# First batch of a Fourier mixer with a maxout FFN: six pieces of weights asked for on ScalarE's DMA queue among the pieces of x

## The chip, the cores and the metric

One core of one Trainium2 chip. The metric is device time in microseconds (us) of one execution of the whole kernel, as the median of several runs.

## What is computed

The inputs are x (8 x 3072 x 256), two mixing matrices and two biases, three up-projections and one output matrix (these four come as 64-bit floats, since they are made by a product of a 32-bit array with a 64-bit scalar). The reference, cut to what matters:

```python
X = np.fft.rfft(x, axis=1)                       # along the 3072 positions
Yr = Xr @ w_r - Xi @ w_i + b_r                   # 256 x 256, complex
Yi = Xr @ w_i + Xi @ w_r + b_i
Y  = sign(Y) * max(|Y| - 0.01, 0)                # both parts apart
y  = np.fft.irfft(Y, n=3072, axis=1).astype(np.float32)
x  = y.reshape(8 * 3072, 256)
h  = max(max(x @ w1, x @ w2), x @ w3)            # 256 -> 768, three times
out = h @ w_out                                  # 768 -> 256
```

## The kernel before

The Fourier transform over 3072 positions is split into a transform over 48 rows and one over 64 columns, with 256 channels kept side by side. The eight batches go through it one after the other; while the tokens of one batch run through the feed-forward part (names pu, pq, pw, pd, most of the kernel's time), the Fourier part of the next is mixed in. Matrices of the main part are split into a high and a low half in 16-bit floats, three products for one.

The **first batch** has nothing to be mixed with, so the kernel begins with its Fourier part alone, in 32-bit floats. This head takes about the first hundred microseconds and has these steps:

- `load_x(q)`, q from 0 to 7 (DMA at L701, for the last piece two halves at L697): one eighth of x, 384 KB, on SyncE's (SP) queue. Only a few tiles are free, so five of the pieces land in parts of tiles that serve later for something else: mb_all twice, wuh, wul and ga_sb; the others in xq_c and xr.
- `stage_a(q)`: two matmuls with the 48-row transform (L746, pa<-x, fr), a copy of half the result by ScalarE (ACT, L747) and of the other half by VectorE (DVE, L748) into a tile `aq` or a borrowed one (wch, wcl, wuh, wul and zq_c stand for aq of pieces 2 to 6), and a store to the scratch a_d in HBM, issued by ScalarE (L749).
- `load_a(k)` (L786, aj<-a_d, on SP's queue): reads rows of a_d across all eight pieces, so the first one waits until all eight stores have landed.
- `first_b(k)`: the 64-column transform (L812, px<-aj, mb_all), copied by ScalarE into tf (L817 and L820). `first_w(k)`: mixing (L838 and L839, py<-tf, wst), then bias and threshold on DVE and ACT (L843 to L849, uf). `first_q(k)`: the first step back (L860, pz<-uf, qf), copied to zs and stored to z_d by ScalarE (L1013, L1014). These three run over 25 values of k.
- after that pi (L1081) reads z_d back as zq_c, scaled and split into zh (ACT, L347) and zl (DVE, L348), and the main part begins.

Meanwhile the **up weights** are prepared. They are twelve pieces of 128 rows x 384 64-bit floats (384 KB each, tile rw), a first half of six and a second half of six. `Weights.load(n, queue=nc.sync)` (L507, its DMA at L515) asks for one on the queue that it is given. `join_half(v)` prepares a half on DVE and ACT: per piece the largest value (L519), the fraction (L549, L552), then, after one exponent for the half is known (a transpose L436 into pt and some small DVE operations, L434 to L534), exponent and combination (DVE L559, ACT L562 into r, DVE L566 and L569). `Mix` then forms differences of the three projections (DVE L622), and splits them in high and low (ACT L342 into wuh, DVE L343 into wul); pieces that are needed the other way round are turned on TensorE (PE) (L575, pt<-id_sb, rw).

What sets the order of work: SP's and POOL's instructions at the head stay in program order. On PE, DVE and ACT a planner in the kernel file orders the instructions of the head by costs and due times when the program is built, `holds` keeping some behind others (`join_half(0)` is called after `stage_a(5)`, and its first PE instruction is held behind that stage's). Each engine then works strictly in that order: an instruction that waits holds up all behind it. Every hardware DMA, from whichever engine it is issued, also takes one of eight completion counters (DMAHW0 to DMAHW7), handed out in turn, and its issue waits until the transfer that had the same counter before has landed.

Of the kernel before, what the change touches and what calls it, by code (L numbers as in the profile page):

```python
# [312 lines left out]
def fourier_maxout_kernel(  # L313
    ctx: ExitStack, tc: tile.TileContext, x, w_r, w_i, b_r, b_i, w1, w2, w3, w_out, fa, ga, mb, mq, ident, out
):
    nc = tc.nc
# [44 lines left out]
    def ff_tile(name):  # L361
        tag = spare[0]
        if len(spare) > 1:
            spare.append(spare.pop(0))
        return ps.tile([P, 512], F32, name=name, tag=tag, bufs=PS[tag])
# [27 lines left out]
    def raw_tile(name):  # L393
        return ffn.tile([P, 768], F32, name=name, tag="raw", bufs=14)
# [18 lines left out]
    def load_first_bias():  # L413
        rows = [b.rearrange("(o d) -> o d", o=1) for b in (b_r, b_i)]
        for j in range(2):
            for c in range(2):
                nc.gpsimd.dma_start(
                    out=bias[64 * c:64 * c + 64, j, :], in_=rows[c].broadcast_to([64, D])
                )
        nc.gpsimd.dma_start(out=bias[64:65, 1, :], in_=rows[0])  # L420
        nc.gpsimd.dma_start(out=qf, in_=mq[:, 0:2])
# [181 lines left out]
    w_up = Weights("u", up_parts, 119.0)  # L603
# [78 lines left out]
    def first_rows(q):  # L682
        return slice(32 * (q % 2), 32 * (q % 2) + 2 * N1)

    def clear(t, rows):
        if rows.start:
            nc.gpsimd.memset(t[0:rows.start], 0.0)

    def load_x(q):
        b, q4 = divmod(q, NCH)  # L690
        xv = x[b].rearrange("(n1 q r n) d -> q r n1 (n d)", n1=N1, r=2, n=4)[q4]
        rows = first_rows(q)
        if q == NCH - 1:
            pairs = [raw_tile("xr")[0:rows.stop, 0:2 * D] for _ in range(2)]
            for c, t in enumerate(pairs):
                clear(t, rows)
                nc.sync.dma_start(out=t[rows], in_=xv[:, :, c * 2 * D:c * 2 * D + 2 * D].rearrange("r n1 d -> n1 r d"))  # L697
        elif b == 0:
            xq = x_homes.pop(0) if q in (0, 1, 4, 5, 6) else xqs[q % 2]
            clear(xq, rows)  # L700
            nc.sync.dma_start(  # L701
                out=xq[rows], in_=x[b].rearrange("(n1 q n) d -> q n1 (n d)", n1=N1, n=8)[q4]
            )
            pairs = [xq[0:rows.stop, c * 2 * D:c * 2 * D + 2 * D] for c in range(2)]
        else:
            xq = xqs[0]
            xqs.reverse()
            if q in (NCH, NCH + 1):
                nc.gpsimd.memset(xq[32:64], 0.0)
            for r in range(2):  # L710
                nc.sync.dma_start(out=xq[64 * r:64 * r + N1], in_=xv[r])
            pairs = [xq[0:XR, c * 2 * D:c * 2 * D + 2 * D] for c in range(2)]
            st["xq", q] = xq[0:XR]
        st["x", q] = pairs
# [470 lines left out]

    for q in range(NCH):
        load_x(q)
        if q == 1:
            nc.sync.dma_start(out=id_sb, in_=ident)
    load_first_bias()  # L1190
    for n in range(6):
        w_up.load(n)
    warm = ff_tile("pt")
    for _ in range(2):
        nc.tensor.matmul(warm, zq[32:64, 0:P], zq[32:64, 0:512], start=True, stop=True)
# [17 lines left out]
    for q in range(NCH):  # L1213
        split_x(q)
        stage_a(q)
        if q == 5:
            placed = nc.cur_bb.bb.instructions
            n = len(placed)
# [51 lines left out]
    for q in (NCH, NCH + 1):  # L1270
        n = len(nc.cur_bb.bb.instructions)
# [94 lines left out]
```

## Time and profile before

| | |
|---|---|
| runs (3) | 1737.45, 1737.54, 1738.77 us; median 1737.54 |
| the profiled execution | 1739.03 us, of which its span 1737.2 us |
| mean granted TensorE clock | 0.992 of full speed |
| PE busy, share of the span | 1684.9 us, 97% |
| DVE, ACT, POOL busy | 75%, 69%, 10% |
| the chain that ended last, by engine | PE 87%, DVE 6%, ACT 3%, issue 2%, DMA 2% |

The span runs from the first to the last instruction of the core; some 1.8 us of the execution's time lie outside it. "Busy" says how long an engine worked at all; the chain of waits says what the end of the program was waiting for, step by step backwards. With PE at 97%, nearly all that is not PE lies in the first 130 us.

### The profile page before, as it was taken

How to read it: one execution, taken by the hardware profiler on the slowest of the kernel's cores; microseconds unless marked ns; L12 is line 12 of the kernel's file. 1: busy time of each engine (PE TensorE's matmuls, PEld its weight loads, DVE VectorE, ACT ScalarE, POOL GpSimd, SP SyncE). 2: the span in 40 equal slices, each digit the busy share in tenths (PEclk: the TensorE clock that was granted, in tenths of full speed). 3: DMA queues.
4: the chain of work that ended last, by engine and by line, in shares of the span. 5: the costliest groups of instructions: out<-in, count | busy, mean ns of one | idle time of the engine just before them, and what ended most of it. 6: DMA issues, size and time to landing. Idle time of an engine off the chain costs nothing.

```text
span 1737.2 us, 38864 instructions
## 1 busy us (share of the span) xinstructions
PE 1684.9 (97%) x15509; PEld 1210.4 (70%) x15509; DVE 1295.3 (75%) x2241; ACT 1198.8 (69%) x2279; POOL 174.8 (10%) x200
## 2 busy tenths in 40 slices
PE   6989999999999999999999999999999999999998
PEld 3856767677676767767776777767777677776676
DVE  5988698678867878678886788768886697856542
ACT  2778687677766877577766777667776677656663
POOL 2000001111011111011111101111101111101110
PEclk8989999999999999999999999999999999999999
DMA  9645353434433433334333444333442233221111
GB/s 307 201 131 164 107 153 90 112 95 125 114 101 101 113 103 107 103 107 121 109 103 87 117 121 120 86 102 108 114 119 83 80 92 86 71 71 37 39 32 32
DMA packets 134996, 185.26 MB, mean 107 GB/s; under 512 B 17776, under 2 KB 113264, under 8 KB 134816
## 3 DMA queue, kind: packets, MB, share of 16 engines
q1 hardware_dynamic: 72784, 106.86, 22.9%
q10 hardware_dynamic: 61824, 75.52, 14.6%
q8 instruction: 122, 2.00, 0.5%
q14 instruction: 58, 0.48, 0.1%
q0 software_dynamic: 208, 0.39, 0.1%
HBM read 87.03 MB, written 75.50 MB: 94 GB/s over the span
## 4 chain that ended last, share of the span: by engine, by line
PE 87%; DVE 6%; ACT 3%; issue 2%; DMA 2%; ACTq 0%; SPq 0%; DVEq 0%
PE pd L353 9%; PE pd L354 9%; PE pd L355 9%; PE pq L353 4%; PE pw L353 4%; PE pw L355 3%; PE pw L354 3%; PE pq L355 3%; PE pq L354 3%; PE pu L353 3%; PE pu L355 3%; PE pu L354 3%; PE pa L756 3%; PE pi L1081 3%; PE py L353 2%; PE py L355 2%
## 5 line engine op out<-in xcount | busy, mean ns | idle before, releaser
L353 PE MATMUL pd<-woh,hh 128*128 128x256 f16 x1152 | 314.1, 273 | 0.6 <-ACT o L1174 0.6
L354 PE MATMUL pd<-wol,hh 128*128 128x256 f16 x1152 | 314.0, 273 | 0.0
L355 PE MATMUL pd<-woh,hh 128*128 128x256 f16 x1152 | 314.0, 273 | 0.0
L1150 DVE SCALAR_TENSOR_TENSOR h<-pq,c 128x384 f32<-128x384 f32 x192 | 106.8, 556 | 163.8 <-PE pq L355 133.5
L343 DVE TENSOR_TENSOR hh<-h,hh 128x768 f16<-128x768 f32 x192 | 189.4, 987 | 37.6 <-ACT hh L342 36.8
L355 PEld LDWEIGHTS <-wul 128*128 128x128 f16 x1344 | 131.3, 98 | 92.3 <-issue 5.5
L353 PEld LDWEIGHTS <-wuh 128*128 128x128 f16 x1344 | 131.3, 98 | 90.3 <-issue 28.4
L354 PEld LDWEIGHTS <-wuh 128*128 128x128 f16 x1344 | 131.4, 98 | 89.1 <-issue 33.6
L342 ACT ACTIVATE hh<-h 128x768 f16<-128x768 f32 x192 | 160.3, 838 | 37.1 <-DVE h L1150 33.0
L1103 POOL TENSOR_TENSOR ys<-yt 128x384 f32<-128x384 f32 x62 | 70.1, 1130 | 1114.2 <-ACT yt L1086 1114.2
L1132 ACT ACTIVATE m<-pw 128x384 f32<-128x384 f32 x192 | 93.8, 489 | 113.2 <-PE pw L355 107.9
L1135 DVE TENSOR_TENSOR pq<-pu,m 128x384 f32<-128x384 f32 x192 | 108.4, 565 | 75.8 <-ACT m L1132 74.4
L1138 ACT ACTIVATE r<-pw 128x384 f32<-128x384 f32 x192 | 94.0, 489 | 98.3 <-PE pw L355 87.9
L353 PE MATMUL pw<-yo,wuh 128*128 128x384 f16 x384 | 125.4, 326 | 12.6 <-ACT m L1132 8.1
L353 PE MATMUL pq<-yo,wuh 128*128 128x384 f16 x384 | 125.3, 326 | 8.1 <-DVE pq L1135 5.4
L354 PEld LDWEIGHTS <-hh 128*128 128x128 f16 x1152 | 112.7, 98 | 27.9 <-issue 0.8
L353 PEld LDWEIGHTS <-hh 128*128 128x128 f16 x1152 | 112.7, 98 | 27.6
L354 PE MATMUL pw<-yo,wuh 128*128 128x384 f16 x384 | 125.1, 326 | 2.4 <-DVE yo L343 2.4
L354 PE MATMUL pu<-yo,wuh 128*128 128x384 f16 x384 | 125.2, 326 | 1.9 <-DVE yo L343 1.9
L353 PE MATMUL pu<-yo,wuh 128*128 128x384 f16 x384 | 125.5, 327 | 0.0
L355 PE MATMUL pu<-yo,wul 128*128 128x384 f16 x384 | 125.2, 326 | 0.0
L355 PE MATMUL pw<-yo,wul 128*128 128x384 f16 x384 | 125.1, 326 | 0.0
(280 smaller groups left out, 4514.8 us busy)
## 6 DMA issues: line engine op xcount, KB each, us to landing
z_d<-zs ACTq DMA_DIRECT2D x96, 256.0 KB, 2.5
out_dram<-o ACTq DMA_DIRECT2D x192, 128.0 KB, 2.4
zq_c<-z_d SPq DMA_DIRECT2D x126, 192.0 KB, 3.4
aj<-a_d SPq DMA_DIRECT2D x90, 256.0 KB, 3.0
xq_c<-in_x_dram SPq DMA_DIRECT2D x112, 192.0 KB, 3.5
a_d<-aq ACTq DMA_DIRECT2D x112, 192.0 KB, 3.0
vq<-vp SPq DMA_DIRECT2D x308, 64.0 KB, 2.3
rw<-in_moe_w_dram SPq DMA_DIRECT2D x12, 384.0 KB, 7.2
```

The lines of the kernel that those rows point to most:

```text
L342: nc.scalar.activation(out=hi, in_=src, func=AF.Copy)
L343: nc.vector.tensor_tensor(out=lo, in0=src, in1=h, op=ALU.subtract)
L353: nc.tensor.matmul(o, lh, rh, start=start, stop=False, **kw)
L354: nc.tensor.matmul(o, lh, rl, start=False, stop=False, **kw)
L355: nc.tensor.matmul(o, ll, rh, start=False, stop=stop, **kw)
L756: nc.tensor.matmul(pa[r][64 * c:64 * c + 64], fr[rows], xs[c][rows], start=True, stop=True)
L1081: nc.tensor.matmul(pi[p][:, o:o + N1], lz[r, n2, h * P:(h + 1) * P], ga_sb[r, lg, c * NQ + n2, :], start=lz is zh and lg == 0, stop=lz is zl,)
L1103: (nc.vector if first else nc.gpsimd).tensor_tensor(out=o, in0=x0, in1=x1, op=op)
L1132: nc.scalar.activation(out=m5, in_=pw, func=AF.Copy)
L1135: nc.vector.tensor_tensor(out=pq, in0=pu, in1=m5, op=ALU.add)
L1138: nc.scalar.activation(out=r1, in_=pw, func=AF.Relu, scale=-H_SCALE)
L1150: nc.vector.scalar_tensor_tensor(out=h32[:, n], in0=o, scalar=scale, in1=c, op0=ALU.mult, op1=ALU.max)
```

## The change

In the loop that asks for the eight pieces of x, each of the first six calls of `load_x` is now followed by a request for one piece of the first half of the up weights, on ScalarE's queue. The loop that asked for the same six on SP's queue, behind all of x and the bias, is gone. Sizes, tiles and arithmetic are the same.

```diff
     for q in range(NCH):
         load_x(q)
+        if q < 6:
+            w_up.load(q, nc.scalar)
         if q == 1:
             nc.sync.dma_start(out=id_sb, in_=ident)
     load_first_bias()
-    for n in range(6):
-        w_up.load(n)
     warm = ff_tile("pt")
```

The planner then orders other engines' work differently as well, up to about 200 us. Behind that PE's order is the same, instruction by instruction, and POOL's is the same throughout. In the listings below, numbers tell tiles of one name apart, and the brackets name the counters that an instruction waits for (DMAHW: a DMA; PE_49, DVE_49 and so on: an engine).

On **ScalarE at the very start**, this is the difference (+ is the changed kernel):

```order
 L1361 UNCONDITIONAL_BRANCH
+L515 DMA rw<-in_moe_w_dram 128x768 x5
 L747 ACT_TABLE_LOAD
 L747 ACTIVATE aq<-pa 96x512
-L749 DMA a_d<-aq 48x2x1024
```

Five of the six requests stand ahead of everything that ScalarE does; the sixth stands behind its first copy. The stores of the eight results pa follow. Before, ScalarE's copies and stores at L747 and L749 stood so:

```order
L747 ACTIVATE aq_142<-pa_143 96x512 [waits PE_49]
L749 DMA a_d_149<-aq_142 48x2x1024 [waits DVE_49,Activation_49]
L747 ACTIVATE aq_151<-pa_152 128x512 [waits PE_49]
L749 DMA a_d_149<-aq_151 48x2x1024 [waits DMAHW1_49,DVE_49,Activation_49]
L747 ACTIVATE wch_76<-pa_159 96x512 [waits PE_49]
L749 DMA a_d_149<-wch_76 48x2x1024 [waits DMAHW3_49,DVE_49,Activation_49]
L747 ACTIVATE wcl_77<-pa_166 128x512 [waits PE_49]
L749 DMA a_d_149<-wcl_77 48x2x1024 [waits DMAHW7_49,DVE_49,Activation_49]
L747 ACTIVATE wuh_78<-pa_173 96x512 [waits PE_49]
L749 DMA a_d_149<-wuh_78 48x2x1024 [waits DMAHW1_49,DVE_49,Activation_49]
```

In the changed kernel:

```order
L747 ACTIVATE aq_142<-pa_143 96x512 [waits PE_49]
L515 DMA rw_116<-in_moe_w2_dram 128x768 [waits DMAHW4_49]
L747 ACTIVATE aq_151<-pa_152 128x512 [waits PE_49]
L749 DMA a_d_149<-aq_142 48x2x1024 [waits DMAHW6_49,DVE_49,Activation_49]
L749 DMA a_d_149<-aq_151 48x2x1024 [waits DMAHW0_49,DVE_49,Activation_49]
L747 ACTIVATE wch_76<-pa_159 96x512 [waits PE_49]
L749 DMA a_d_149<-wch_76 48x2x1024 [waits DMAHW3_49,DVE_49,Activation_49]
L747 ACTIVATE wcl_77<-pa_166 128x512 [waits PE_49]
L749 DMA a_d_149<-wcl_77 48x2x1024 [waits DMAHW7_49,DVE_49,Activation_49]
L747 ACTIVATE wuh_78<-pa_173 96x512 [waits PE_49]
L749 DMA a_d_149<-wuh_78 48x2x1024 [waits DMAHW3_49,DVE_49,Activation_49]
L747 ACTIVATE wul_79<-pa_180 128x512 [waits PE_49]
```

The first store moved behind the second copy, and the store of wuh now waits for counter 3, which the store of wch uses two stores ahead of it, where it waited for counter 1.

On **DVE around the two last copies of stage a** (zq_c for piece 6, aq_266 for piece 7), before:

```order
L519 TENSOR_REDUCE mwu_93<-rw_119 128x1
L549 TENSOR_SCALAR m5_188<-rw_119 128x384
L552 SCALAR_TENSOR_TENSOR rw_119<-rw_119,m5_188 128x384
L748 COPY zq_c_86<-pa_260 96x512
L519 TENSOR_REDUCE mwu_93<-rw_121 128x1
L559 TENSOR_SCALAR c1_223<-rw_119 128x384
L549 TENSOR_SCALAR m5_192<-rw_121 128x384
L748 COPY aq_266<-pa_268 128x512
```

In the changed kernel (the pieces of weights are rw_97, rw_101, rw_105, rw_109, rw_112 and rw_116):

```order
L559 TENSOR_SCALAR c1_235<-rw_105 128x384
L748 COPY zq_c_86<-pa_260 96x512
L566 SCALAR_TENSOR_TENSOR r1_224<-rw_97,r1_224 128x384
L569 SCALAR_TENSOR_TENSOR rw_97<-rw_97,r1_224 128x384
L566 SCALAR_TENSOR_TENSOR r1_230<-rw_101,r1_230 128x384
L559 TENSOR_SCALAR c1_241<-rw_109 128x384
L566 SCALAR_TENSOR_TENSOR r1_236<-rw_105,r1_236 128x384
L569 SCALAR_TENSOR_TENSOR rw_101<-rw_101,r1_230 128x384
L748 COPY aq_266<-pa_268 128x512
L569 SCALAR_TENSOR_TENSOR rw_105<-rw_105,r1_236 128x384
```

Between the two copies stand now three combinations of weights (L566), two L569 and one L559, where one maximum, one exponent mask and one fraction stood.

On **ScalarE between the last two stores of stage a and the first tf**, before:

```order
L749 DMA a_d_149<-zq_c_86 48x2x1024 [waits DMAHW7_49,DVE_49,Activation_49]
L747 ACTIVATE aq_266<-pa_267 128x512 [waits PE_49]
L347 ACTIVATE qh_71<-qf_70 128x256 [waits DMASW5_49]
L749 DMA a_d_149<-aq_266 48x2x1024 [waits DMAHW3_49,DVE_49,Activation_49]
L562 ACTIVATE r1_224<-c1_223,bwu0_221 128x384 [waits DVE_49]
L562 ACTIVATE r1_230<-c1_229,bwu0_221 128x384
L562 ACTIVATE r1_236<-c1_235,bwu0_221 128x384 [waits DVE_49]
L817 ACTIVATE tf_296<-px_291 128x4x128 [waits PE_49]
L820 ACTIVATE tf_296<-px_291 128x4x64
```

In the changed kernel:

```order
L749 DMA a_d_149<-aq_266 48x2x1024 [waits DMAHW6_49,DVE_49,Activation_49]
L562 ACTIVATE r1_242<-c1_241,bwu0_221 128x384
L562 ACTIVATE r1_248<-c1_247,bwu0_221 128x384 [waits DVE_49]
L347 ACTIVATE qh_71<-qf_70 128x256 [waits DMASW5_49]
L562 ACTIVATE r1_254<-c1_253,bwu0_221 128x384 [waits DVE_49]
L342 ACTIVATE wuh_78<-rw_109 128x384 [waits DMAHW3_49,DVE_49]
L342 ACTIVATE wuh_78<-rw_112 128x384 [waits DMAHW1_49,DVE_49]
L342 ACTIVATE wuh_78<-rw_116 128x384 [waits DVE_49]
L342 ACTIVATE wuh_78<-rw_97 128x384 [waits DVE_49]
L342 ACTIVATE wuh_78<-rw_101 128x384 [waits DVE_49]
L817 ACTIVATE tf_296<-px_291 128x4x128 [waits PE_49]
L820 ACTIVATE tf_296<-px_291 128x4x64
```

Three more r (L562), and five splits wuh<-rw (L342), which before came after the first tf's, stand ahead of the first tf now.

## Rows read from the trace of the kernel before

**Rows 1.** The page's first line: the span of the profiled execution.
```profile
span 1737.2 us, 38864 instructions
```
**Rows 2.** Chain of waits, 15 to 50 us: start us, us, what.
```profile
15.19 6.96 DMA a_d<-wch
...
27.01 5.66 DMA a_d<-aq
32.69 2.58 DMA aj<-a_d
35.40 3.76 PE px L812 x16
39.16 0.68 PE py L838 x2
...
42.86 0.89 PE px L812 x8
...
49.18 0.43 PE py L838 x2
```
**Rows 3.** Windows: us, PE, PEld, DVE, ACT, POOL busy (count), PEclk, DMA share, GB/s.
```profile
5.00:10.00 5.00, 4.65 (x6) 1.63 (x6) 0.40 (x1) 0.59 (x1) 2.67 (x5) 1.00 1.05 261
23.00:25.00 2.00, 0.14 (x1) 0.00 (x0) 1.99 (x5) 0.29 (x1) 0.00 (x0) 1.00 1.03 415
25.00:30.00 5.00, 0.00 (x0) 0.00 (x0) 4.54 (x12) 0.61 (x2) 0.00 (x0) 0.59 1.03 385
...
39.20:100.00 60.80, 60.80 (x306) 50.61 (x309) 57.98 (x175) 43.87 (x86) 0.94 (x1) 1.00 0.55 184
105.00:110.00 5.00, 1.38 (x10) 0.53 (x3) 5.00 (x12) 3.49 (x8) 0.00 (x0) 0.78 0.74 184
110.00:115.00 5.00, 4.25 (x22) 3.60 (x20) 5.00 (x12) 2.38 (x4) 0.00 (x0) 0.50 0.82 203
```
**Rows 4.** DMA queues, 3 to 15 us: packets, MB, share of 16 engines.
```profile
q1 hardware_dynamic: 955, 2.85, 92.7%
q0 software_dynamic: 128, 0.26, 8.9%
```
**Rows 5.** DMA issues at 10.4 and 72.9 us: count, KB, us from issue to landing.
```profile
a_d<-aq ACTq DMA_DIRECT2D x1, 384.0 KB, 7.3
...
z_d<-zs ACTq DMA_DIRECT2D x1, 256.0 KB, 2.1
```
**Rows 6.** ScalarE in order of time, 24 to 38 us: start us, us, line, out<-in [idle before].
```profile
24.13 0.54 ACTq L749 DMA_DIRECT2D a_d<-zq_c  x1
24.71 0.60 ACT L747 ACTIVATE aq<-pa 128x512 f32<-128x512 f32 x1 [2.05 <-DMA a_d<-wcl]
...
37.49 0.60 ACT L817 ACTIVATE tf<-px 128x512 f32<-128x512 f32 x1 [2.25 <-PE px L812]
```
**Rows 7.** Waits of SP, 0 to 45 us: us in total, times, longest.
```profile
SPq L515 <- DMA a_d<-wch: 5.9, 1, 5.9
```
**Rows 8.** DVE in order of time, 34 to 48 us.
```profile
34.51 0.55 DVE L566 SCALAR_TENSOR_TENSOR r<-rw,r 128x384 uint32<-128x384 uint32 x1
34.98 0.35 DVE L559 TENSOR_SCALAR c<-rw 128x384 uint32<-128x384 uint32 x1
...
47.32 0.55 DVE L519 TENSOR_REDUCE mwu<-rw 128x1 f32<-128x384 f32 x1 [0.48 <-DMA rw<-in_moe_w_dram]
```
**Rows 9.** DVE and PE in order of time, 114 to 121 us, and ScalarE's zh before it.
```profile
111.70 1.15 ACT L347 ACTIVATE zh<-zq_c,s0u 112x1024 f16<-112x1024 f32 x1
...
114.27 1.28 DVE L348 SCALAR_TENSOR_TENSOR zl<-zq_c,s0u,zh 112x1024 f16<-112x1024 f32 x1
...
115.60 0.22 PE L1081 MATMUL pi<-ga_sb,zl 48*128 48x48 f16 x2 [0.69 <-DVE zl L348]
116.59 2.93 PE L575 MATMUL pt<-id_sb,rw 128*128 128x128 f32 x12
120.31 0.26 PE L1081 MATMUL pi<-ga_sb,zh 48*128 48x48 f16 x4
```

## The prediction
> **What bounds the kernel now.** I read the page's busy shares first, then the chain of waits, then windows, then single engines in order of time. The span is 1737.2 us [rows 1] and PE is busy in 97% of it, so a change at the head can only move what PE loses there. From 39.2 to 100 us PE is busy 60.80 of 60.80 us [rows 3], with DVE busy in 57.98 of them: whatever delays the first py is still there at 100 us, since nothing in that stretch can be made up. Two places have slack: the time before the first py, and 105 to 120 us, where PE is busy 1.38 and 4.25 of 5 us while DVE is busy all the time [rows 3].
>
> The chain before the first py [rows 2] is one of transfers: a store of stage a, the last store a_d<-aq (asked for at 27.01, landed 32.67), the first aj (2.58), px from 35.40, py from 39.16. The windows say why a store took 5 to 7 us: the DMA share is 1.05 and 1.03, so all engines move data without a break [rows 3], x at 261 GB/s and weights and stores at 415. A piece of 384 KB (393 KB in thousands) is so worth 1.5 us as x and 0.95 as a weight or a store.
>
> In which order transfers move decides the case. The first store a_d<-aq, on ScalarE's queue, took 7.3 us [rows 5] from its issue at 10.4, and from 3 to 15 us the queue q10 (ScalarE's) has no row at all: only SP's q1 and POOL's q0 moved bytes [rows 4]. That store waited for pieces of x that had been asked for before it. With an empty queue a store of 256 KB takes 2.1 us [rows 5]. So I take transfers to move in the order in which they were asked for, whichever queue they are on.
>
> **The change, part by part.**
>
> *Six requests on ScalarE instead of SP.* An issue takes about 0.55 us of the engine [rows 6]. Five stand ahead of all that ScalarE does, but it has nothing to copy before the first piece of x has landed and been transformed: free. SP loses six issues, among them one that waited 5.9 us for a store's counter [rows 7], so SP is free earlier: nothing, because what it asks for next (mb_all, wst) is used only from px on.
>
> *The weights' bytes move ahead of x and the stores.* The store of wch landed at 15.19 + 6.96 = 22.15 [rows 2], and two of the six weight pieces had moved before it. Now all six stand ahead: four pieces more, 4 x 0.95 to 1.0, so it lands at about 26.2. The total of bytes is the same, so this alone would cost nothing for the last store; what makes it cost is a counter. In the changed order of ScalarE the store of wuh waits for counter 3, which the store of wch holds. The engine works in order, so at 26.2 it still has this to do: store wuh 0.55, copy wul 0.60, store 0.55, one r 0.60, copy zq_c 0.60 (durations: [rows 6], r as a copy). DVE's half of zq_c stands behind an L559 that waits for that r (28.5), so it is ready at about 29.6; store zq_c until 30.2, two more r until 31.45. DVE has six weight instructions between its last two copies; the third L566 waits for the r of 31.45, and then L566, L569 and the copy (0.47 apart [rows 8], the copy about 0.7, an estimate from ScalarE's 0.60 for the same shape) end at 33.2. The last store goes out at 33.2 instead of 27.01. By then the queue is empty: 2.1 [rows 5] and 0.35 for the larger piece, landed 35.7 (before 32.67); plus 2.58 for aj, px starts at **38.3, 3.0 later**.
>
> *tf behind five splits.* Before, tf stood only behind px (it waited 2.25 us for it [rows 6]). Now five wuh<-rw stand in front, and the last of them needs DVE's weight work up to its difference L622: 18 instructions behind the copy of 33.2, 0.47 apart and the two L559 among them 0.3 [rows 8], 8.2 us; then the split. tf starts at 41.9 instead of 37.49, and the first py as long after it as before (39.16 - 37.49, less the 0.6 for which py waited on px's end), at 42.95 to 43.2: **4.0 later**. px lies beside this and costs nothing.
>
> *The exponent of the second half.* pt (L436) now stands before the first pz instead of behind the px that follows it. It needs the maximum of the last piece of the second half, which came in at 47.3 [rows 8]; SP asks for it behind the aj's, so some 3 later, 50.3. With the small steps behind it, the py that stood at 49.18 [rows 2] starts at 53.7: **4.5 later in all**, and that goes on to 100 us.
>
> *The clock.* From 25 to 30 us PE has no work and the granted clock is 0.59 on average, on its way to 0.50 of full speed, the lower of the two levels (1.2 GHz) [rows 3]. So 16 px took 3.76 us where 8 take 0.89 later, and the return came at about the end of px: the first two py took 0.68 us, two later ones 0.43 [rows 2]. Now px ends at 42.1 and PE waits 0.9 us before py. From 110 to 115 us PE was busy 4.25 of 5 us and the clock stayed at 0.50 [rows 3], so such gaps can hold it down. Lowest cost: nothing, if it returns as early after px starts as before. Highest: 4.6, if it stays down until the gap at pt is past (9.2 us at half speed). The row with gaps is the nearest one: about 4 us of py at half speed, **+2**.
>
> *The end of the head.* About 10 us of DVE work on the first half is done before py instead of beside it. From 105 to 115 us DVE is busy all the time [rows 3]. The first zl (114.27) starts 1.4 us after its zh has ended (111.70 + 1.15) because wcl, wol and sd stand before it [rows 9]: up to 1.4, taken as 1.1. Between the first and the second pi stand turns of weights, 2.93 us from 116.59 [rows 9]; the second zl, 117.89 + 1.28 [rows 9], holds the second pi back to 119.2 anyway, and it starts at 120.31: 1.1. Together **-2.3**. Bounds: -0.5, if zh alone sets the time, and -5, if PE has no long gap at 105 and so keeps its clock up.
>
> **Sum:** 4.5 + 2 - 2.3 = 4.2. The profiled execution took 1739.03 us, 1.8 of it outside the span, so it would take 1743.2; the median of the runs is 1.5 below it, 1737.54, which gives 1741.7. A measurement of this kernel tells 0.2%, 3.5 us, from no change, so the bounds are 1734.0 and 1741.0.
>
> **Rivals.**
>
> *The two queues share the engines.* Then weights beside x take half the rate from the start, but stores are not held behind x: the store of wch lands at about 20, and ScalarE is no longer bound by the counter but by piece 6 of x. That lands when seven pieces at 1.5, six weights at 0.95 and 1.5 us of tables and bias have moved from 3 us on, 20.7, and its copy follows 2 us later, 22.9 with its matmuls. All of the above comes 3.3 us earlier: 4.5 - 3.3 + 2 - 2.3, about 1738.5, no change that can be told. Against it stand 7.3 us for the first store and the missing q10 [rows 4, 5]: it moved nothing while SP's queue had work. The Trainium skill ("DMA: Bandwidth & Descriptors", Queues, rings and completion order) says that each DMA engine goes round between the queues that have work; by that rule this rival is the forecast, and the trace does not agree before 15 us. The same page (Issuing engines are not separate DMA queues) says that issuing from several engines saves only issue time, which speaks against a gain from the second queue; no row here contradicts that. 0.2.
>
> *DVE's relief decides; the time falls.* The mechanism is the stretch 105 to 120. If the planner's shift takes enough weight work off DVE there that the first pi follows its zh at once and PE never idles 2 us, the clock stays up: at 110 to 120 some 8.6 us of PE work ran at half speed, of which most would be saved, 4 us, beside the 2.3. It decides where the delay of the first py is under 2.5 us, thus where the last store goes out by about 30.5 (as it would if the wait for counter 3 ended three us earlier). Then 1.0 to 2.5 - 2.3 - 4: about 1733. For it: DVE busy all through that stretch [rows 3]. Against it: the gap at 105 to 110, PE busy 1.38 of 5 [rows 3], is a round trip of z_d through HBM, which no DVE work is part of. 0.17.
>
> *The clock stays down for all of the first py's.* As the highest price above: 2.6 more, 1744.3. For it, the 0.50 from 110 to 115; against it, PE has no gaps from 39.2 on [rows 3]. 0.13.
>
> *Nothing changes.* The pieces land early, but the chain of stores through x is as it was, with the order's effects cancelling: about 1737.5. Against it the counter, which stands in the order. It shares the middle with the first rival; 0.1 beside the 0.2.
>
> **How the numbers follow.** Forecast 0.4, spread of its terms -2 to +1.5 us on each, so that about a fifth of it falls under 1741.0. Slower: 0.32 + 0.13 = 0.45. Within 0.2%: 0.08 from the forecast, 0.2 and 0.1 = 0.38. Faster: 0.17. The range from 1734.0 to 1745.0 leaves out most of the third part of the cases on the fast side and the longest of the clock's. The likeliest case alone, slower, spans 1740 to 1744.5.
>
> **What would show it.** Right: the store of wch lands at 26 and the store of wuh is issued just then; the last store of stage a is issued at 33 (before 27.0); the first aj lands, and px starts, at 38 (35.4); five splits stand before tf, at 42 (37.5); the py of 49.18 starts at 53.7; q10 moves the weights early and in turn with x; a row of granted clock below 1.00 behind 43 us. At the end zl follows its zh at once. Wrong: stores that land within 3 us of their issue while x still moves (then the queues share); a last store before 30 us; px's start within 1 us of before; or PE with less idle time between 105 and 120 us than the 2.3 us allow.

## The result, and the profile after

The changed kernel is slower: median 1747.53 us over 4 runs (1746.54 to 1749.54) beside 1737.55 us for the kernel before (4 runs, 1737.45 to 1738.77); ratio 1.0056, 95% interval [1.0041, 1.0072]. The medians are 10.0 us apart; the profiled execution took 1748.35 us, 9.3 more than that of before. The forecast was 1741.7, with a range up to 1745.0: the direction was right, the size was not.

One correction to the description ahead: the steps first_b, first_w and first_q run over 12 values of k, not 25. No number rests on it.

The page of the changed kernel begins (compare [rows 1]):

```profile
span 1746.6 us, 38866 instructions
```

Its chain of waits over the first 60 us (start us, us, what; compare [rows 2]):

```profile
0.73 4.48 DMA rw<-in_moe_w_dram
5.23 11.94 DMA xq_c<-in_x_dram
...
17.31 10.46 PE pa L746 x16
...
35.67 3.28 DMA a_d<-aq
...
54.83 0.49 PE pt L436 x2
...
57.07 0.43 PE py L838 x2
```

The chain now begins with a weight and waits 12 us for a piece of x, and pa stands on it with 10.46 us. The last store goes out at 35.67 (27.01 before), and the py that stood at 49.18 stands at 57.07, 7.9 later.

Windows of the changed kernel (columns as in [rows 3]):

```profile
5.00:10.00 5.00, 1.27 (x2) 0.39 (x2) 2.47 (x6) 1.28 (x1) 2.71 (x5) 1.00 1.04 263
10.00:15.00 5.00, 5.00 (x8) 1.70 (x6) 2.02 (x5) 1.19 (x2) 0.00 (x0) 1.00 1.05 277
...
19.00:21.00 2.00, 2.00 (x4) 0.82 (x3) 0.00 (x0) 0.59 (x1) 0.00 (x0) 0.50 1.04 304
45.00:50.00 5.00, 5.00 (x20) 4.28 (x20) 4.38 (x12) 1.96 (x5) 0.00 (x0) 0.70 1.05 392
110.00:115.00 5.00, 4.72 (x30) 3.04 (x30) 3.21 (x14) 3.33 (x7) 0.00 (x0) 1.00 0.63 184
...
130.00:140.00 10.00, 8.66 (x31) 2.80 (x28) 6.43 (x9) 6.10 (x11) 0.00 (x0) 0.50 0.65 172
```

and, of the kernel before, one window that was not shown and the queues of a window that was (23 to 25 us):

```profile
130.00:140.00 10.00, 9.79 (x105) 4.69 (x103) 8.88 (x13) 8.80 (x18) 0.00 (x0) 1.00 0.67 182
...
q10 hardware_dynamic: 226, 0.79, 97.7%
q1 hardware_dynamic: 18, 0.04, 5.4%
```

Three things stand in these rows. From 5 to 15 us the DMA engines are as full as before, but move 263 to 277 GB/s although about half of it is weights, which alone moved at 374 (e6 below). The 415 GB/s of 23 to 25 us, at which the prediction priced a weight [rows 3], were stores: 0.79 of 0.83 MB came from ScalarE's queue. From 19 to 21 us TensorE does stage a at half speed. And at the end of the head the lower clock has moved: before it lay on 110 to 115 us [rows 3], now these are at 1.00 and the lower clock lies on 130 to 140, on 8.66 us of TensorE's work, most of it feed-forward matmuls.

The queues of the changed kernel from 3 to 15 us (compare [rows 4]), and the issue of its first store at 14.4 us (compare [rows 5]):

```profile
q10 hardware_dynamic: 663, 1.81, 51.7%
q1 hardware_dynamic: 566, 1.40, 44.2%
q0 software_dynamic: 128, 0.26, 8.1%
...
a_d<-aq ACTq DMA_DIRECT2D x1, 384.0 KB, 9.3
```

Both queues move bytes in turn, yet a store still takes 9.3 us behind x and weights. SP was not freer for its six requests less: its requests for x stood 5.8 us behind counters that weights held, which the prediction did not count (the DMA engines were full all the same).

ScalarE and DVE between 28 and 45 us (start us, us, line, out<-in; compare [rows 6]):

```profile
28.52 0.54 ACTq L749 DMA_DIRECT2D a_d<-wuh  x1
...
34.92 0.68 DVE L748 COPY aq<-pa 128x512 f32<-128x512 f32 x1
...
35.67 0.54 ACTq L749 DMA_DIRECT2D a_d<-aq  x1
...
44.36 0.57 ACT L817 ACTIVATE tf<-px 128x512 f32<-128x512 f32 x1
```

The store of wch went out at 21.81 and landed 6.6 us later, at 28.4; the store of wuh follows it at once, as the counter in the order says. DVE's last copy ends at 35.60, TensorE had its operand ready at 31.4: the copy came over 3 us later, behind the weight instructions between the two copies.

TensorE at the places that the runs below compare (compare [rows 9]):

```profile
17.31 7.01 PE L746 MATMUL pa<-xq_c,fr 96*96 96x512 f32 x8 [2.14 <-DMA xq_c<-in_x_dram]
...
41.98 2.05 PE L812 MATMUL px<-mb_all,aj 128*128 128x128 f32 x8 [10.57 <-DMA aj<-a_d]
...
45.53 1.06 PE L838 MATMUL py<-wst,tf 128*128 128x256 f32 x2
...
109.97 1.12 PE L860 MATMUL pz<-uf,qf 128*128 128x512 f32 x2 [1.16 <-DVE mxu L849]
...
115.95 1.68 PE L575 MATMUL pt<-id_sb,rw 128*128 128x128 f32 x12 [1.18 <-DVE wcl L580]
118.09 1.68 PE L575 MATMUL pt<-id_sb,rw 128*128 128x128 f32 x12 [0.47 <-DVE wcl L580]
120.39 0.97 PE L575 MATMUL pt<-id_sb,rw 128*128 128x128 f32 x6 [0.61 <-DVE mb_all L580]
121.39 0.22 PE L1081 MATMUL pi<-ga_sb,zh 48*128 48x48 f16 x4
...
130.06 0.50 PE L353 MATMUL pu<-yo,wuh 128*128 128x384 f16 x1
```

The kernel before has the first py, the last pz and the first pu here:

```profile
38.95 0.89 PE L838 MATMUL py<-wst,tf 128*128 128x256 f32 x2
...
102.08 1.12 PE L860 MATMUL pz<-uf,qf 128*128 128x512 f32 x2 [1.16 <-DVE mxu L849]
...
122.41 0.34 PE L353 MATMUL pu<-yo,wuh 128*128 128x384 f16 x1
```

The first py starts 3.55 us behind px in both: the five splits in front of tf cost it nothing. The 9.3 us arise in four stretches: px 41.98 - 35.40 = 6.6; px to the last pz 1.3 more (109.97 - 102.08 = 7.9); pz to the first pu 20.09 beside 20.33, 0.2 back; pu to the end of the span 1616.5 beside 1614.8, 1.7 more.

### The profile page after: what moved, and what is told of

Its sections match the earlier page's. It is cut to its first block, busy times and chain, and to the rows that moved or that the text cites. A ratio compares the mean times of both kernels' runs of the same rounds, so it can differ in the third digit from the quotient of the medians.

```text
span 1746.6 us, 38866 instructions
## 1 busy us (share of the span) xinstructions
PE 1691.5 (97%) x15509; PEld 1209.8 (69%) x15509; DVE 1296.4 (74%) x2241; ACT 1199.5 (69%) x2279; POOL 176.2 (10%) x200
## 4 chain that ended last, share of the span: by engine, by line
PE 86%; DVE 6%; ACT 4%; issue 2%; DMA 2%; ACTq 0%; SPq 0%; DVEq 0%
PE pd L353 9%; PE pd L355 8%; PE pd L354 8%; PE pq L353 4%; PE pw L353 4%; PE pw L355 3%; PE pw L354 3%; PE pq L355 3%; PE pq L354 3%; PE pu L353 3%; PE pu L355 3%; PE pu L354 3%; PE pa L756 3%; PE pi L1081 3%; PE py L353 2%; PE py L355 2%
## 5 line engine op out<-in xcount | busy, mean ns | idle before, releaser
L342 ACT ACTIVATE hh<-h 128x768 f16<-128x768 f32 x192 | 160.4, 838 | 36.1 <-DVE h L1150 32.8
```

Of the source, the lines that this page charges most:

```text
L342: nc.scalar.activation(out=hi, in_=src, func=AF.Copy)
```

## The experiments

Each kernel ran beside the kernel before, whose medians in the four groups of runs were 1737.98 to 1738.79; the ratio is to those of its own group. px, the last pz and the first pu are TensorE's starts in the profiled execution, "span" is its span. One execution of each kernel was profiled, and its time is not always near the median.

| kernel | px | last pz | first pu | span | median us | ratio, 95% interval |
|---|---|---|---|---|---|---|
| before | 35.40 | 102.08 | 122.41 | 1737.2 | 1737.55 | |
| changed | 41.98 | 109.97 | 130.06 | 1746.6 | 1747.53 | 1.0056 [1.0041, 1.0072] |
| e1 both on SP | 39.00 | 106.89 | 125.42 | 1744.6 | 1747.73 | 1.0049 [1.0034, 1.0064] |
| e2 prepared behind x | 38.66 | 106.16 | 126.00 | 1745.1 | 1746.15 | 1.0038 [1.0023, 1.0053] |
| e3 two pieces | 36.81 | 105.09 | 127.37 | 1745.7 | 1744.15 | 1.0029 [1.0017, 1.0041] |
| e4 ScalarE, behind stages | 37.44 | 104.19 | 123.84 | 1738.3 | 1740.28 | 1.0017 [1.0007, 1.0026] |
| e5 all late | 32.23 | 103.31 | 125.60 | 1742.9 | 1744.45 | 1.0034 [1.0021, 1.0046] |
| e6 weights first | 40.62 | 109.13 | 128.56 | 1746.8 | 1748.09 | 1.0059 [1.0044, 1.0074] |
| e7 extra pa | 41.11 | 113.43 | 133.72 | 1752.6 | 1748.74 | 1.0067 [1.0047, 1.0087] |
| e8 before, extra pa at 105 | 35.30 | 102.95 | 124.74 | 1740.0 | 1740.74 | 1.0017 [1.0007, 1.0026] |
| e9 turns doubled | 41.80 | 110.34 | 131.00 | 1746.7 | 1748.95 | 1.0068 [1.0051, 1.0085] |
| e10 two late | 34.58 | 104.46 | 123.76 | 1740.9 | 1742.75 | 1.0026 [1.0016, 1.0036] |
| e11 e2 and e7 | 37.75 | 105.38 | 125.13 | 1743.1 | 1747.65 | 1.0051 [1.0037, 1.0065] |
| e12 turns as before | 40.63 | 108.58 | 126.37 | 1740.7 | 1743.98 | 1.0028 [1.0017, 1.0039] |
| e13 e2 and e12 | 39.02 | 106.15 | 124.42 | 1738.0 | 1740.89 | 1.0011 [1.0001, 1.0020] |

### Bytes or queue

**e1**, the changed kernel with `w_up.load(q)` in place of `w_up.load(q, nc.scalar)`.

> The six weight pieces asked for at the same places of the loop, but on SP's queue. Theory 1 (the bytes ahead of x are the cost, not the queue): x still ends late, its last half at 25 to 28 us instead of 17.9, the first px at 38 to 42 instead of 35.4, and the time is 1742 to 1748. Rival (sharing between two queues is the cost): with one queue x and weights move in order without loss; x's last half at 24 to 25, px within 2 us of before, time 1737 to 1740.

x ended later still: its last half was asked for at 22.71 and took 6.6 us, 29.3 (27.7 in the changed kernel: 19.32 and 8.3). px came 3.6 late, not within 2, and the time is that of the changed kernel: what moves ahead of x costs on either queue. But the loss does not lie where it lay. px is 3.0 earlier than in the changed kernel, although x ended 1.6 later: the planner put one combination of weights between DVE's last two copies, where the changed kernel has six weight instructions, and the last store went out at 32.86. That was lost again behind the first pu, 1619.2 us to the end beside 1616.5. The granted clock was 0.50 there from 130 to 135 us, and for some 3 us more at 348 and at 1573 us:

```profile
130.00:135.00 5.00, 4.67 (x17) 1.35 (x16) 2.38 (x2) 1.93 (x3) 0.00 (x0) 0.50 0.59 159
```

**e4**, the requests on ScalarE's queue, but in the second loop:

```diff
         stage_a(q)
+        if q < 6:
+            w_up.load(q, nc.scalar)
```

> The six requests on ScalarE's queue, but each behind the stage of its own piece of x; the planner puts two of them ahead of the first stores and four behind the last store. If the queue is innocent and only the bytes' place counts: x is late by one or two pieces (last half at 19 to 20.5), the last store at 27 to 28, px at 34 to 36, and the four late pieces delay the end of the head by 1 to 3 us: 1738 to 1742, clearly below the changed kernel. If a request on ScalarE's queue in itself holds its stores up: px at 38 or later, 1744 and more.

1740.28, as expected if the queue itself does not cost, and clearly below the changed kernel. px, at 37.44, fits neither expectation (34 to 36, or 38 and more). Only two of the six pieces move ahead of the stores here, so this run says less of the bytes than of the requests.

**e6**, the kernel before with all six pieces asked for on SP ahead of the first x.

> All six weight pieces asked for on SP's queue ahead of the first piece of x, so that weights and x do not alternate. Theory M (alternating weights with x makes the weights' bytes move at x's rate): unmixed, the six weights are in by 9 to 10 us at 0.95 each and x ends at 24 to 25 (before 17.9 plus six), earlier than the 27.7 of the changed kernel and the 29.3 of the run with both on SP. Theory N (the early microseconds are slow whatever moves): x ends at 27 to 29 here too. The time is 1741 to 1748 either way, since px comes 4 to 7 late.

Theory M holds. Windows of e6, the first with weights alone:

```profile
4.00:9.00 5.00, 1.51 (x2) 0.00 (x0) 3.92 (x10) 0.00 (x0) 3.77 (x7) 1.00 1.00 374
14.00:19.00 5.00, 5.00 (x7) 1.95 (x8) 0.77 (x2) 0.59 (x1) 1.08 (x2) 1.00 1.04 264
```

Weights alone move at 374 GB/s in the same early microseconds, and x ends at 24.4 (17.09 and 7.3), 3.3 to 4.9 us before the runs in which the two alternate. So a weight piece among x costs what x costs or a little more (x's end moved by 9.8 us for six pieces in the changed kernel, 1.6 each), and ahead of x, unmixed, 1.1. The time is no better for it: the first x lands later, stage a begins at 13.96, and the store of wcl goes out at 27.30 (25.90 in the changed kernel).

**e3**, two of the six pieces as in the change (`if q < 2`), four as before.

> Only the first two pieces of weights on ScalarE's queue beside x, the other four on SP behind x as before. Theory 1: x is late by two pieces, 2 to 3 us (last half at 20 to 21 instead of 17.9), and the last store by no more, since DVE and ScalarE work in an order close to the one before: 1737 to 1740. Theory 2: with the order of the engines as before nearly the whole loss is gone: 1736.5 to 1738. If one third of the bytes costs one third of the time: 1741.

A miss: px is only 1.4 late, yet the median is 5.4 us above its own runs of before. A third of the bytes costs over half the loss. In the profiled execution, the slowest of six, most of it arises behind px: 3.0 at the last pz, 5.0 at the first pu, 8.5 at the end. As in the changed kernel, all eight turns of weights stand ahead of the first pi, and the lower clock lies on the feed-forward part behind them:

```profile
130.00:140.00 10.00, 9.18 (x31) 3.20 (x30) 5.44 (x7) 4.79 (x9) 0.00 (x0) 0.50 0.55 140
```

### The order of DVE and ScalarE, and the clock in stage a

**e2**, the changed kernel with `if q == NCH - 1` for `if q == 5` around `join_half(0)`.

> The change as it is, but the first half's preparation is held behind the last piece of x instead of the sixth, so that no exponent or combination of weights stands between the last copies of stage a on DVE and ScalarE. Theory 1 (late bytes): x lands as in the changed kernel (last half 27.7), px comes at most 1 us earlier than 41.98, time 1746 to 1748. Theory 2 (order of the engines): the last store goes out at 32 to 33 instead of 35.67, px at 39, tf right behind px, and 3 to 4 us of the 10 come back: 1743 to 1745.

The last store goes out at 31.29 and px at 38.66, 3.3 earlier, as theory 2 said; tf stands right behind px again. Half the loss at px is thus the order of the two engines together with stage a's clock, which stayed at 1.00 in this trace; against e12, where it stayed at 1.00 too (below), the order alone is 2.0 (1.6 in e13). The rest is put down to the late bytes. In the time only 1.4 of it is seen (3 to 4 were expected), and the intervals overlap: the rest is lost behind pz.

**e7**, the two pa of the second piece done twice, so that TensorE has no gap before the third; the planner counts the second pair as nothing.

```diff
-            for c in range(2):
-                nc.tensor.matmul(pa[c][0:n], ..., xs[c], start=True, stop=True)
+            for c in range(4 if q == 1 else 2):
+                nc.tensor.matmul(pa[c % 2][0:n], ..., xs[c % 2], start=True, stop=True)
```

> The changed kernel with the two matmuls pa of the second piece of x done twice (same result), counted by the planner as nothing so that no order moves: TensorE then has no 2 us gap before the third piece. If the lower clock from 17.3 us on is part of the loss: the next four pa take 3.6 us instead of 7.0, the last pa ends at 29.5 instead of 31.4, the last store goes out 1 to 2 us earlier and so does px (40 to 41): 1745.5 to 1746.5. If the counters and DVE's order alone set the last store: px at 41.5 to 42 and no change, 1747 to 1748.

The clock stays at 1.00 and the last pa starts at 26.84 instead of 29.53, but px gains 0.9 only, the counters and DVE being next. A later wait of 3 us, for the second half's exponent, takes it back in this execution, the slowest of four:

```profile
55.45 0.80 PE L436 MATMUL pt<-id_sb,col 128*128 128x128 f32 x2 [3.01 <-DVE col L434]
```

That the added work held the clock is not shown: e12 below has the changed kernel's order on every engine up to px and no work added, and in its profiled execution stage a ran at 1.00 as well,

```profile
19.00:21.00 2.00, 1.83 (x5) 0.54 (x4) 2.00 (x5) 0.00 (x0) 0.67 (x2) 1.00 1.01 371
```

with px at 40.63, 1.4 earlier. So the lower clock in stage a costs about 1 us at px, and differs between executions. **e11**, e2 and e7 together:

> The changed kernel with both remedies: preparation held behind the last piece of x, and the two extra pa that keep TensorE at work before the third piece. Loss at px by parts: order of the engines 2.4, lower clock in stage a 0.9, late bytes 3.3 of 6.6. So px at 38 to 39 and the rest of the head as in the run with the first remedy alone; 1744 to 1746.5. If bytes were not the rest, px would come within 1 us of 35.4.

px 37.75, last pz 105.38, about as the parts add up to; the time, 1747.65, does not follow (1744.86, the profiled execution, to 1748.47).

### The end of the head

**e9**, four of the eight turns on TensorE (L575) done twice, to fill the gaps from 114 us on.

> The changed kernel with four of the eight turns on TensorE done twice (0.8 us each), which fills most of the gaps between 113.8 and 121.4 us, counted as nothing by the planner. Theory C: the clock no longer falls at 123 and the 15.6 us of work that ran at half speed until 140 run at full speed; 7 us less half-speed loss, 1 to 1.5 us added: 1742 to 1744. Rival: the clock falls anyway or the gaps are bound by DVE, and the added work costs 1 us: 1748 to 1749.

Half a miss. The clock does stay up, as this window of e9 shows:

```profile
120.00:125.00 5.00, 4.10 (x34) 3.68 (x34) 3.91 (x5) 2.51 (x4) 0.00 (x0) 1.00 0.53 137
```

but each turn waits for the copies of the one before, so the added work went onto the chain: first pi at 124.35 instead of 121.39. No time was won (1748.95, the rival's price). **e8** did the same to the kernel before, with the pa of batch 1's second piece four times.

> The kernel before, with the matmuls pa of the second piece of batch 1 done four times (same result), counted by the planner as nothing: 3.3 us of work that fills the 3.62 us gap from 105.9 us. Theory C (the lower clock at the end of the head costs time): the clock stays at 1.00 from 107.8 to 121.5, where 10.6 us of work ran at half speed; 2 to 4 us less, 1734.5 to 1737. Rival (DVE and the trip of z_d through HBM set the time there): same within 0.5 us, or up to 1 us more from the work added.

The rival was right that nothing is won, but put the price too low: the clock fell anyway, 5 us later (113.1), the first pu came 2.3 us late and the median is 2.8 above its own runs of before, where at most 1 was expected.

**e12**, the changed kernel with three of the eight turns held behind the first pi, TensorE's order of before:

```diff
-    for n in (0, 1, 6, 7, 4, 5, 10, 11):
+    for n in (0, 1, 6, 7, 4):
         turns[n][0]()
...
     halves.append(inverse(0, 0))
+    done = nc.cur_bb.bb.instructions
+    last = next(i.name for i in done[::-1] if str(i.engine).endswith("PE"))
+    for n in (5, 10, 11):
+        at = len(done)
+        turns[n][0]()
+        holds += [(last, i.name) for i in done[at:] if str(i.engine).endswith("PE")]
     split_z(0)
```

> The changed kernel with three of the eight turns held behind the first pi, which is the order of TensorE before. Theory T (the turns ahead of pi hold up pi and spread TensorE's work so thin that the clock falls on the pa and pu behind it): px still at 42, but first pi 2 us earlier against px, the stretch from the first pu to the 200th pd 112 us as before instead of 114.4, and 3 to 4 us less: 1743.5 to 1745. Rival (the trip of z_d sets pi, and the clock falls as it did): pi and pu as in the changed kernel within 0.5 us, 1746.5 to 1748.5.

Theory T holds in the time: 1743.98, 3.5 below the changed kernel (4.7 when each is taken beside its own runs of before), the intervals apart. Its pi comes 0.9 us earlier against px, not 2. TensorE in e12:

```profile
119.18 0.22 PE L1081 MATMUL pi<-ga_sb,zh 48*128 48x48 f16 x4 [2.94 <-ACT zh L347]
...
126.37 0.34 PE L353 MATMUL pu<-yo,wuh 128*128 128x384 f16 x1
```

and its clock:

```profile
120.00:125.00 5.00, 4.50 (x88) 4.32 (x90) 2.20 (x5) 3.13 (x5) 0.00 (x0) 0.66 0.62 185
...
130.00:140.00 10.00, 9.35 (x58) 4.24 (x57) 7.95 (x18) 8.48 (x18) 0.00 (x0) 1.00 0.61 170
```

pz to pu is 17.79 (20.33 before, 20.09 changed): TensorE waits 2.94 us idle for zh, and still the pu is earlier, since the turns come between the two pi, where it would wait anyway; and the lower clock is over before the feed-forward part. Of the 2.3 us, 0.8 lie ahead of the first pi and 1.5 behind it; pu to the end is 2.2 shorter than in the changed kernel. The 1.4 by which px is earlier is not the edit's.

The other traces bear this out. In the 18 us from the first pu the granted clock is 0.64 to 0.91 in the seven kernels that have all eight turns ahead of the first pi (changed, e1, e2, e3, e6, e7, e11). It is 1.00 in those that do not (before, e4, e8, e10, e12, e13; 0.97 in e5), and in e9, where turns are doubled.

**e13**, e12 and e2 together: TensorE's order is then that of before but for one transpose.

> The changed kernel with that order of the turns and with the preparation held behind the last piece of x: TensorE's order is that of before but for one transpose, and only the early bytes of the weights remain. If bytes, order of DVE and ScalarE, and order of the turns are all there is: px at 38.7, last pz 4 late, end of the head as before or 1 us shorter, 1740.5 to 1742.5. If lateness alone moves the lower clock onto other work: 1744 to 1746.

1740.89, as expected, so lateness alone does not move the lower clock; its slowest run (1741.94) is below the fastest of e12 (1742.50). Beside the runs of before of its own group the loss is 10.0 us with all, 5.3 with the turns put back, 2.2 with the preparation on DVE and ScalarE put behind the last copies too. The 2.2 that are left are put down to the early bytes by exclusion: the requests on ScalarE's queue, their counters and what still differs in the two engines' orders are in them, and no run parts these.

### The other direction

**e5**, the kernel before with the six requests, and the first half's preparation, moved behind `load_a(FIRST[0])`; **e10**, the same for two of the six.

> The opposite of the change: all six pieces asked for on SP behind the first load of stage a's results, and the first half prepared after that. If transfers of weights in front of the stores are what holds px back, also before: the last store goes out at 25 and lands at 27 to 28, px starts at 30 instead of 35.4. Theory A (the head is a chain of transfers): up to 5 us less, 1732 to 1735. Theory B (DVE is full from 39 to 100 us, and the work it did before 39 us now lies in that stretch): PE waits there for DVE, and the gain is given back, 1736 to 1742.

> The kernel before, with two of the six pieces asked for on SP behind the first load of stage a's results (and the first half's exponent taken after that), a smaller step than all six. Theory A (transfers set px): 2 us of bytes fewer ahead of the last store and no wait for a late weight's counter; it goes out at 25.5 to 26, px starts at 32 to 33.5 instead of 35.4. Theory B: what is gained at px comes back at the end of the head, where the first half's turns wait for their combinations (with all six late: px 3.2 earlier, the first pu 3.2 later). With a third of the pieces late B gives back 1 to 3 us: 1735.5 to 1739; without B 1734.5 to 1736.

Both times the gain is given back, as theory B said, but by more than its range (1744.45 against 1736 to 1742, 1742.75 against 1735.5 to 1739), and not by DVE between 45 and 100 us, where TensorE is busy throughout in e5. With all six late px comes 3.2 earlier. TensorE then waits 2.2 us for the next loads of stage a's results (aj and ajq, at 41 and 43.7), the last pz is 1.2 late, and at the end of the head TensorE waits 7.6 us for zh, so that the first pu is 3.2 late. With two late px gains only 0.8 (its store still took 5.7 us), and the wait at the end, for the copies of a turn, is 7.5:

```profile
114.68 0.26 PE L1081 MATMUL pi<-ga_sb,zh 48*128 48x48 f16 x4 [7.60 <-ACT zh L347]
...
115.72 1.65 PE L575 MATMUL pt<-id_sb,rw 128*128 128x128 f32 x6 [7.48 <-DVE wcl L580]
```

The first line is from e5, the second from e10. No run beat the kernel before.

## Why the prediction was wrong in size

**Held.** The direction, and its first mechanism: weights ahead of x and the stores make the last store late, through counter 3 (store of wuh at 28.52, when that of wch landed) and through DVE's weight work between the copies. The pt for the second half did delay pz (0.3 us), and PE was full up to the last pz, so that the head's loss went on. The rival with two sharing queues failed in what it was to bring: both queues moved in turn (51.7% and 44.2%), but a store did not come through earlier for that (9.3 us). That the engines go round between the queues is what the Trainium skill ("DMA: Bandwidth & Descriptors", Queues, rings and completion order) states. With one queue (e1) x was no earlier; that fits what the same page of the Trainium skill says under "Issuing engines are not separate DMA queues".

**Failed 1: "four pieces more, 4 x 0.95 to 1.0".** The price came from a stretch in which stores moved almost alone. Among x a piece costs 1.5 to 1.6 us (e6 against the changed kernel), so the store of wch landed at 28.4 and not at 26.2. The last store then went out at 35.67 and not at 33.2 and took 3.3 us and not 2.45, and px came 6.6 late and not 3.0. Since x came in slowly, TensorE had a gap of 2.1 us before the third piece, and in this execution it then did four pa at 0.50, in 7.0 us instead of 3.6 (e13, with a gap of 1.9 us there, stayed at 1.00). The prediction had no term for stage a's own clock. It is worth about 1 us at px, in the executions that have it.

**Failed on the way: "px lies beside this and costs nothing".** The prediction let the five splits set tf and the first py, 4.0 late. They stood there, but with px 6.6 late they held tf up by 0.3 only and py not at all: py follows px by 3.55 us as before, so it is 6.6 late, all of it px's.

**Sized wrong: "about 4 us of py at half speed, +2".** The lower clock lay on the first 2.5 us of py (0.70 in 45 to 50 us); with the pt it gave 1.3 between px and the last pz, where the prediction had 2.5. The head as a whole was forecast at 6.5 and took 7.9. That this is so close is luck: the first py was forecast 2.6 too early, and what follows it 1.2 too late.

**Failed 2: "Together -2.3" at the end of the head.** (Its two terms, 1.1 each, make 2.2.) The relief is real: e12 has it, pz to pu 17.8 instead of 20.3. But the prediction read it on the order of before. With the weights ready early the planner puts all eight turns ahead of the first pi; zh starts 10.2 us behind the last pz, behind their copies on ScalarE, where it starts 9.4 behind it in e12, as its load lands; and TensorE works through a chain of turns with gaps. ScalarE in the changed kernel and then in e12:

```profile
119.81 0.49 ACT L579 ACTIVATE mb_all<-pt 128x384 f16<-128x384 f32 x1 [0.22 <-PE pt L575]
120.20 1.14 ACT L347 ACTIVATE zh<-zq_c,s0u 112x1024 f16<-112x1024 f32 x1
...
117.98 1.15 ACT L347 ACTIVATE zh<-zq_c,s0u 112x1024 f16<-112x1024 f32 x1 [1.21 <-DMA zq_c<-z_d]
```

That took back the 2.3, and moved the lower clock from the turns and pi onto the feed-forward part; pu to the end is 1.7 us more. Of the 5.1 us between forecast and measurement (4.2 and 9.3 in the profiled executions) the head is about 1.4 and this step about 3.8.

**Open.** Why x moves at 261 GB/s and drags the weights along when they alternate was not tried. Runs of one kernel were up to 7 us (e3) and 8 us (e7) apart, those of before 2 to 3; what differs between such runs was not followed up. The record shows one thing that does: the mean granted clock, 0.987 in e3's run of 1747.49 us and 0.992 in that of 1740.62. The traces of e1, e2, e3, e4 and e6 each have one or two stretches of some 3 us at 0.50 far behind the head, near 348 or 1570 us; those of the kernel before and the changed one have none there. So parts that are read from single traces hold to some 1 to 2 us, an estimate: 3.4 us at half speed cost 1.7. Why the clock falls on the work behind a row of short turns is open too.

## What to carry to other kernels

A transfer's price holds only beside the neighbours it was measured with: price it in the stretch where it will move, with what will move beside it. Where a planner sets the order, work that becomes ready earlier is also put in earlier, so read the new order at the far end too, at each place where the old one left an engine room to wait; over a third of this loss (e12) lay 80 us behind the change. And an engine's spare time is worth something only if what fills it is not in front of the critical step.

## What the runs showed of the hardware

- Weights of 384 KB moved at 374 GB/s ahead of x (e6, 4 to 9 us), stores at 415 (before, 23 to 25 us), x at 261 to 264; weights and x alternating, both together at 263 to 277.
- Work added on TensorE to keep the clock up cost at least what the clock gave: doubled turns, each of which waits for the copies of the one before, put the first pi 3.0 us later (e9), and 3.3 us of pa put the first pu 2.3 later and did not hold the clock (e8).
- TensorE left idle 2.9 us at 116 us (e12) and 3.0 us (e13) ran the feed-forward stretch from 130 to 140 us at 1.00, after 3.4 us at 0.50, while the same stretch behind a row of short turns (changed kernel) ran at 0.50: where the clock falls depended on how the gaps lay, and its price on what stood in the stretch.
